# Unit 0's MoE in two halves of 128 tokens, more filler matmuls, other engines for some steps, and a new order table

## The chip, the cores and the metric

One core of a Trainium2 chip runs the whole kernel. The metric is the device time in microseconds (us) of one execution; several executions give a median. Engines are named as the profile names them: PE is TensorE (matmuls; PEld its weight loads), DVE VectorE, ACT ScalarE, POOL GpSimd, SP SyncE, which here issues the DMAs.

## The reference

For each of 4 batches and 8 heads a complex decaying state of 48 by 48 runs over 768 steps; then a feed-forward layer ("MoE" in the code) works on the joined heads.

```
scale = minimum(mag, 0.999) / (mag + 1e-06)      # mag = |a_re + i a_im|
a_re_n, a_im_n = a_re * scale, a_im * scale
for t in range(S):
    S_re, S_im = ar*S_re - ai*S_im + k_t v_t^T, ar*S_im + ai*S_re
    y[t] = q_t . S_re
x = y.transpose(0, 2, 1, 3).reshape(B * S, H * D)    # 3072 x 384
h = x @ w_in                                      # 384 -> 2048
g = h * tanh(softplus(h))
out = g @ w_out                                   # 2048 -> 384
```

## The kernel before

**Units.** The 3072 tokens are cut into 12 units of 256 tokens (three per batch), each of two chunks of 128. A unit passes four stages.

**Elementwise** (`elementwise`, L298 to L468): loads of R and I (real and imaginary decay), Q, K and V; then magnitude and phase of the decay. ScalarE does squares ("size r", "size i"), logs, exponentials, arctan and sines, VectorE the sums, the running sums over time ("scan", L391, L406), the clamp of the slope to +-1.5 (L383) and the products with q and k ("grow" L423, "turn" L447). Twelve "relay" DMAs per unit (L454) then carry the turned q and k to the layout T of the attention. Units 0 and 1 do this in two groups, one per chunk. ScalarE's functions come from two tables; `Work.act` (L161) loads the other one (an ACT_TABLE_LOAD at L164) whenever the order asks for it.

**Attention** (`attention`, L472 to L597), chunk by chunk: "kn" transposes k (L497), "am" forms the masked products (L509, L516), "y" the output in PSUM (L527), "y out" copies it to SBUF (L532), "pd", "S add" and "S fade" carry the state. Four "x move" DMAs (L577) then bring a unit's y to x, the input of the MoE; from unit 1 on x is split in a high and a low part, xH and xL (L587, L592).

**MoE** (`moe`, L599): the 2048 columns are 8 pairs of 2 x 128. For each pair "mm1" (L609) makes h in PSUM (128 partitions x 2 x 256 tokens); ScalarE does exp, square, ln and an inverse exp, VectorE a cap (L668) and the gate (L621); "mm2" (L644) adds the pair's part to two PSUM tiles po, one for each 128 tokens. In unit 0 both are plain fp32 matmuls; from unit 1 on each is three fp32r matmuls of high and low parts (gh, gl at L627, L633), with weights split likewise. "o0", "o1" copy po out and two stores from SP end the unit (L655 to L661).

**Weights** (`weight`, L240): 16 blocks (w_in and w_out of each pair by turns) come as 64-bit words in two buffers; "low" on ScalarE, "shift" and "join" on VectorE and "carry" (L264, POOL or VectorE) make fp32 of them. A block's buffer is free for the next but one after its carry. `halves` (L274) splits them for units 1 to 11 ("high", "rest").

**Order.** Each step is an operation `op(engines, name, f)`, numbered in the order in which the program lists it. The table ORDER (L49) holds these numbers in the order in which the operations are issued, with a letter where another of the allowed engines than the first is taken. Each engine, and SP's queue, works through its operations strictly in this order, so one that waits holds up all behind it. Unit 0 is listed with six "spin" operations of four matmuls of a constant (L685), whose result nobody reads.

Of the kernel before, what the change touches and what calls it, by code (L numbers as in the profile page):

```python
# [26 lines left out]
P = 128  # L27
# [3 lines left out]
C = 128  # L31
# [7 lines left out]
PLAIN = 1  # L39
SPINS, SPIN = 6, 4  # L40
# [12 lines left out]
545 136 95 91 304 132 97 133 96 99 98 93 134 305 94 135 101 324 306 542 337A 106 334 137 141 336 335 108 338 100 340  # L53
103 543 102 342 344 343 104 341 143 142 347 109 107 544 144 345 346 409 115 110 145 541 325 105 407 113 329 116 326
111 327 138 114 405 112 330 363 413 351 365 117 364 366V 367 331 352 139 349 201 348 368 140 353 546 202 350 371 203
146 151 212 355 339 411 359 358 211 357 551 204 547 361 205 221 360 213 332 548 362 206 222 214 719 147 148 720 356
549 215 369 153 207 149 216 374 552 208 150 118 217 370 152 119 375 218 223 372 154 550 156 376 224 155 554 379 120
225 209 380 226 161 377 232 158 378 417 559 159 210 227 354 157 406 539 219 724 540 160V 162 163 381 166 220 228 553
164 382 727 383 555 165 419 385 560 415 231 384 725 386 726 390 556 171 233 242 167 168 557 241 234 169 235 558 391
392 170V 243 229 172 173 176 244 569A 570A 236 174 230 245 561 393 175 237 562 246 238 423 373V 239 247 181 563 177  # L60
248 387 421 564 425 251 178 566 568 565 388 183 252 723 179 182 911 184 240 180 567 572 389 249 253 395 397 250 396
427 186 398 399 185V 575 573 401 254 261 429 402 191 579 577 255 574 262 256 576 187 188 582 400 257 189 580 263 585
403 258 190 581 264 259 578 192 583 260 910 196 193 265 584 404 266 586 194 588 587 408 267 195 590 589 268 918 592
410 915 269 916 271 197 198 433 591 272 199 917 593 437 273 200V 450 274 435 412 449 275 394 276 414 595 277 728 594
278 733 438 416 596 730 461 439 451 418 270 734 452 735 420 279 453 736 440 454 737 462 441 455 729 280 442 738 443
597 281 283 599 282 444 739 284 598 474 445A 600 731 463 446 473 732 456 464 447 457 601 475 448 458 741 459 422 740
460 476 465 424 752A 477 486 466 571 426 722 751A 602 478 721 431V 467 428 604 479 468 485 603 497 605 487 469 488 498
470 489 742 480 490 471 750 499 472 491 606 481 500 482 501 607 743 502 483 503 430 914 608 484 744 612 434 609 510
745 610 611 509 492 748 504 747 522 493 505 494 521 615V 506 749 495 616 754 511 496 507 432 756 613 617 757 523 512
# [3 lines left out]
777 931 646 629 782 778 934 780 647 935 784 930 786 783 630 648 638 787 936 656 649 639 944A 785 943 650 667 1107 640  # L73
# [3 lines left out]
695 688 800 960 1117 962 799 1105 689 1114 696 1104 1119 808 690 1106 697 806V 809 804 807 1115 698 704 805 699 703  # L77
700 963 1124 810 1125 961 705 701 1126 1127 823 1128 1118 706 1129 1289 822 1120 707 811 1130 1121 964 966 708 965 702
967 968 812 709 813 969 1123 710 814 971 711 712 970 973 815 972 713 974 824 975G 816 825 976 1122 978 714 979 1133
1131 835 826 1476 715 834 1135 827 977V 716 1134 717 817 980 828 718 1137 836 847 1132 829 982 1138 818 1139 846 837  # L80
1290 819 1141 1144 1142 858 1140 820 1143 838 981 1145 848 821 830 1146 839 983 1147 1291 831 859 1150 849 840 1136
1294 1148 832 850 1149 1483 841 833 1475 851 1296 842 860 871 1293 852 1297 1287 853 987 1286 861 989 854 843 985 862
988 1306 1298 1151 984 1295 870 855 1288 863 1307 990 882 1308 991G 986 872 995 1309 1153 864 844 993 1299 873 992
1310 845 874 994 1300 1301 856 865 875 1302 866A 857 876 867 996 894 998 877 1000 1312 999 868 878 1001 879 895 997
1303 1480 1003 1152 1481 869 1154V 1311 883 1305 1484 880 884 1486 896 1002 1304 897 885 1155 898 1316 1317 1315 886
1157 899 887 881 1156 900 1158 888 1162 1319 1313 1164 1482 1160 1668 1314 889 1320 1159 901 1321 890 1014 1322 1161V
1004 1163 1015 1165 902 891 1026 903 1016 1005 1489 892 1017 1166 1018 1326 893 1325 1006 1324 1019 904 1323 1007 1485
1329 1020 905 1008 1318 1332 1487 1490 1328 1027 1331 906 1492 908 1167 907 1009 1491 909 1327 1010A 1039 1493 1330
1028 1488 1667 1011 1038 1021 1012 1494 1478 1022A 1013 1477 1040 1023 1051 1168 1497 1029 1024 1496 1041 1498 1030
# [4 lines left out]
1182 1678 1090 1073 1681 1183 1081 1184 1334 1336 1082A 1185 1091 1083 1682 1197 1092 1684 1084 1186 1093 1683 1187  # L94
1085 1094 1188 1685 1674 1196 1095 1189 1686 1208 1190 1198 1209 1199 1687 1677 1096 1200 1679 1688 1337 1201 1339
1700A 1338 1680 1097 1340 1344 1098 1689 1690 1346 1100 1099 1202 1101 1341 1191 1342 1347 1345 1221 1192 1348G 1343
1691 1210 1220 1524 1193 1349 1351 1522 1211 1350 1194 1203 1352 1523 1212 1692 1517 1353 1222 1515 1204 1213 1223
1232 1516 1354 1224 1670 1205 1214 1357 1225 1669 1693 1215 1699A 1355 1226 1694 1854 1195 1227 1857 1356 1206 1696
1216 1228 1695 1207 1217 1701 1218 1698G 1229 1697 2041 1219 1855 1233 1244 1234 1702 1858G 1230 1856 1231 1235 1358
1245 1863 1359V 1236 1709 1360 1246 1362 1237 1257 1366 1238 1361 1247 1365 1363 1248 1525 1239 1527 1368 1249 1256  # L100
1364 1367 1859 1240A 1704 1250 1268 1241 1705 1369 1258 1861 1269 1712 1370 1862 1710 1371V 1373V 1242 1372 1671 1259
2040 1374 1711 1251 1243 1260 1703 1526V 1270 1528V 1375 1252 1860 1529 1261 1253 1531 1864 1530 1376 1271 1262 1532
1272 1263 1536 1865 1866 1538 1273 1537 1867 1388 1377 1274 1378 1264A 1387 1539 1275 1540G 1379 1265 1276A 1400 1389
1380 1533 1390 1868 1381 1541 1391 1543 1399 1392 1542V 1544 1871 1254 1869 1870 1872 1545 1873 1393 1255 1882 1874
1546 1266 1875 1277 1267 1877 1876 1278 1878 1279 1879 2233 1547 1280 1552 1282 1382 1281 1283 1534 1383 1401 1384
# [96 lines left out]
def tile_kernel(ctx, tc, q, k, v, are, aim, w_in, w_out, out):  # L202
# [38 lines left out]
    def weight(i):  # L241
# [9 lines left out]
        def low(e):  # L251
            act(word(0).bitcast(I32), word(0), AF.Copy, scale=2.0 ** -29)
# [40 lines left out]
    def wout(x, j, a):  # L293
        return x[2 * j + 1].rearrange("p (a c) -> p a c", a=2)[:, a, :]

    units = {}

    def elementwise(u):  # L298
        b, uu = divmod(u, NU)
        split = u < SPLIT_UNITS  # L300
# [171 lines left out]
    def attention(u):  # L472
# [109 lines left out]
        if u < PLAIN:  # L582
            return
# [310 lines left out]
```

## Time and profile before

| | us |
|---|---|
| median of 3 runs | 625.02 (623.94 to 625.76) |
| the profiled execution | 623.0 |
| its span, first to last instruction | 621.3 |
| PE busy | 568.6 (92%) |
| ACT busy | 507.4 (82%) |
| DVE busy | 482.2 (78%) |
| POOL busy | 42.9 (7%) |

The profiled execution is 1.7 us longer than its span (what lies around the instructions), and lies 2.0 us under the median. "Busy" counts the time in which at least one instruction ran on the engine. Matmuls are pipelined, so a busy PE need not be at its peak; their ends are modelled. The mean granted clock of the PE was 0.988 of full speed.

### The profile page before, as it was taken

Reading aid. Unit: us, or ns where it says so; the run is one execution under the profiler, and the core shown is the slowest. Engines: PE = TensorE matmul, PEld = TensorE weight load, DVE = VectorE, ACT = ScalarE, POOL = GpSimd, SP = SyncE. Lnnn points to the kernel's source line nnn. Section 1 sums busy time; section 2 is a strip of 40 time slices with the busy share of each in tenths; the row PEclk is TensorE's granted clock in tenths of the full one; section 3 lists DMA queues with packets and bytes.
Section 4 is the critical chain, followed back from the end, with each engine's and each line's share of the span. In section 5 each row is a group of like instructions: output and inputs, shape, how many; then the busy total and the mean of one; then the engine's idle time right before and its main releaser. Section 6 shows DMA issues by size and latency. Waiting matters only on the chain.

```text
span 621.3 us, 11450 instructions
## 1 busy us (share of the span) xinstructions
PE 568.6 (92%) x4394; PEld 532.8 (86%) x4394; DVE 482.2 (78%) x836; ACT 507.4 (82%) x804; POOL 42.9 (7%) x38
## 2 busy tenths in 40 slices
PE   0268987899999999999999999999999999999996
PEld 0256665689999989999999999999999999999995
DVE  5999898799998889899887976987984555353542
ACT  8999998687899999999998986899975755344780
POOL 1032231200000000000003000001000000000000
PEclk9998999799999999999999999999999999999999
DMA  8387757702543517063332433351160021020000
GB/s 292 124 245 209 210 192 221 188 26 73 130 131 94 162 61 208 15 177 114 95 100 64 119 95 111 108 142 60 47 169 16 1 78 27 1 53 1 26 1 31
DMA packets 56222, 65.46 MB, mean 105 GB/s; under 512 B 4704, under 2 KB 49760, under 8 KB 56160
## 3 DMA queue, kind: packets, MB, share of 16 engines
q1 hardware_dynamic: 56160, 64.65, 36.0%
q8 instruction: 36, 0.59, 0.4%
q14 instruction: 26, 0.21, 0.1%
HBM read 36.18 MB, written 4.72 MB: 66 GB/s over the span
## 4 chain that ended last, share of the span: by engine, by line
PE 38%; ACT 31%; DVE 15%; DMA 8%; issue 4%; SPq 3%; DVEq 0%; ACTq 0%
PE ph L609 15%; PE po L644 14%; ACT e L166 10%; ACT X L166 7%; ACT L164 6%; PE pa L509 3%; PE ypsum L527 3%; DMA T<-QK 3%; DMA x<-y 2%; DVE g L621 2%; SPq L454 2%; PE pd L539 2%; ACT R L166 2%; DMA I<-a_im 1%; DVE gl L633 1%
## 5 line engine op out<-in xcount | busy, mean ns | idle before, releaser
L609 PE MATMUL ph<-xH,wh 128*128 128x256 f32 x462 | 134.6, 291 | 1.7 <-DVE g L621 1.6
L609 PE MATMUL ph<-xL,wh 128*128 128x256 f32 x462 | 130.1, 281 | 0.0
L609 PE MATMUL ph<-xH,wl 128*128 128x256 f32 x462 | 129.8, 281 | 0.0
L166 ACT ACTIVATE e<-e 128x512 f32<-128x512 f32 x192 | 117.3, 626 | 12.6 <-DVE e L668 11.5
L644 PE MATMUL po<-wh,gh 128*128 128x384 f32 x308 | 106.7, 347 | 0.0
L644 PE MATMUL po<-wh,gl 128*128 128x384 f32 x308 | 104.7, 340 | 0.5 <-DVE gl L633 0.5
L644 PE MATMUL po<-wl,gh 128*128 128x384 f32 x308 | 104.3, 338 | 0.0
L609 PEld LDWEIGHTS ph<-xH,wh 128*128 128x128 f32 x462 | 87.2, 189 | 5.3 <-issue 1.7
L609 PEld LDWEIGHTS ph<-xL,wh 128*128 128x128 f32 x462 | 87.1, 189 | 0.2
L609 PEld LDWEIGHTS ph<-xH,wl 128*128 128x128 f32 x462 | 87.2, 189 | 0.0
L166 ACT ACTIVATE e<-ph 128x512 f32<-128x512 f32 x96 | 56.2, 591 | 32.5 <-PE ph L609 31.6
L164 ACT ACT_TABLE_LOAD x63 | 80.8, 1283 | 1.1
L621 DVE SCALAR_TENSOR_TENSOR g<-e,ph 128x512 f32<-128x512 f32 x96 | 65.0, 682 | 19.6 <-ACT e L166 18.3
L633 DVE TENSOR_TENSOR gl<-g,gh 128x512 fp32r<-128x512 f32 x88 | 60.6, 691 | 19.2 <-PE po L644 10.4
L668 DVE TENSOR_SCALAR e<-e 128x512 f32<-128x512 f32 x96 | 42.5, 443 | 36.2 <-ACT e L166 35.7
L166 ACT ACTIVATE e<-e,fifth 128x512 f32<-128x512 f32 x96 | 68.4, 719 | 1.1
L644 PEld LDWEIGHTS po<-wh,gh 128*128 128x128 f32 x308 | 57.9, 188 | 1.5 <-issue 1.5
L644 PEld LDWEIGHTS po<-wh,gl 128*128 128x128 f32 x308 | 57.9, 188 | 1.4 <-DVE gl L633 1.2
L644 PEld LDWEIGHTS po<-wl,gh 128*128 128x128 f32 x308 | 57.9, 188 | 0.0
L509 PE MATMUL pa<-T 96*128 96x128 f32 x384 | 51.2, 283 | 1.7 <-ACT kn L502 1.7
L509 PEld LDWEIGHTS pa<-T 96*128 96x128 f32 x384 | 48.1, 197 | 3.3 <-ACT kn L502 2.4
L497 PE MATMUL pkn<-ident,T 96*128 96x96 f32 x160 | 18.6, 255 | 29.4 <-DMA T<-QK 28.2
(102 smaller groups left out, 1054.9 us busy)
## 6 DMA issues: line engine op xcount, KB each, us to landing
T<-X SPq DMA_DIRECT2D x72, 129.0 KB, 2.5
T<-QK SPq DMA_DIRECT2D x72, 129.0 KB, 2.5
words<-w_in SPq DMA_DIRECT2D x8, 768.0 KB, 4.9
words<-w_out SPq DMA_DIRECT2D x8, 768.0 KB, 5.7
V<-v SPq DMA_DIRECT2D x12, 384.0 KB, 4.2
QK<-k SPq DMA_DIRECT2D x12, 384.0 KB, 4.5
QK<-q SPq DMA_DIRECT2D x12, 384.0 KB, 4.8
out_dram<-o SPq DMA_DIRECT2D x24, 192.0 KB, 2.3
```

What stands on the lines that cost most here:

```text
L164: self.nc.scalar.preload_act_table_set(need)
L166: return self.nc.scalar.activation(out, in_, func, **kw)
L454: e.dma_start(to[part * NJ + j], st[src][:, c, j])
L497: e.transpose(d["pkn", g][:, i, :], T()[:, 4 * g + i, 1, :C], ident)
L509: e.matmul(d["pa", g][:, i, :], T()[:, 4 * g + i, 1, :C], T()[:, 4 * g + i, 0, :C], start=True, stop=True)
L527: e.matmul(ypsum[64 * par:64 * par + D, i, :], lhs, rhs, start=m == 0, stop=first or m == 1)
L539: e.matmul(d["pd", g][:, i, :], d["kn"][:, h, :], st["V"][:, c, h * D:(h + 1) * D], start=True, stop=True)
L609: e.matmul(ph[j][:, a, :], win(x, j, kt, a), st[y][:, kt, :], start=n == 0, stop=n + 1 == len(todo))
L621: e.scalar_tensor_tensor(g_[j], e_[j], 2.5, ph[j], ALU.subtract, ALU.mult)
L633: e.tensor_tensor(gs[j][1], g_[j], gs[j][0].bitcast(F32), ALU.subtract)
L644: e.matmul(po[t], x[:, a, t * P:(t + 1) * P], wout(y, j, a), start=j == 0 and a == 0 and n == 0, stop=j + 1 == NPAIR and a == 1 and n + 1 ...
L668: op("V", f"{n} cap", lambda e, j=j: e.tensor_scalar_min(e_[j], e_[j], math.exp(20.0)))
```

## The change

The diff, without the order table and the parts that only pass names along:

```
-PLAIN = 1
-SPINS, SPIN = 6, 4
+PLAIN = (8, 0)
+HALVED = (0,)
+SPINS, SPIN = 40, 2
...
         def low(e):
-            act(word(0).bitcast(I32), word(0), AF.Copy, scale=2.0 ** -29)
+            if e is nc.scalar:
+                act(word(0).bitcast(I32), word(0), AF.Copy, scale=2.0 ** -29)
+            else:
+                e.tensor_scalar(word(0).bitcast(I32), word(0), 2.0 ** -29, None, ALU.mult)
...
-        op("A", f"w{i} low", low)
+        op("AV", f"w{i} low", low)
...
-                op("A", f"{n} size r", size_r)
+                op("AV", f"{n} size r", size_r)
...
-                op("A", f"{n} size i", lambda e: act(half(1), I(), AF.Square, scale=0.5))
+                op("AV", f"{n} size i", size_i)
...
-                op("V", f"{n} clamp", lambda e: e.tensor_scalar(I(), I(), -1.5, 1.5, ALU.max, ALU.min))
...
-                op("V", f"{n} turns", lambda e: e.tensor_scalar(I().bitcast(I32), x1(), INV2PI, None, ALU.mult))
+                op("VA", f"{n} turns", lambda e: act(I().bitcast(I32), x1(), AF.Copy, scale=INV2PI) if e is nc.scalar
+                   else e.tensor_scalar(I().bitcast(I32), x1(), INV2PI, None, ALU.mult))
...
-            op("A", f"{n} abs", lambda e: act(R(), I(), AF.Abs))
+            op("AV", f"{n} abs", lambda e: act(R(), I(), AF.Abs) if e is nc.scalar
+               else e.tensor_scalar(R().bitcast(U32), I().bitcast(U32), 0x7FFFFFFF, None, ALU.bitwise_and))
...
-        banks = dict(kn=("ph", 3), am=("pa", 2), pd=("po", 2)) if u == 0 else dict.fromkeys(("kn", "am", "pd"), ("pa", 2))
+        banks = {"kn": ("ph", 3) if u == 0 else ("pa", 2), "am": ("pa", 2), "pd": ("pa", 2)}
...
+        def move(ts, p0, j, r0, n):
+            def f(e):
+                y = st["y"][r0:r0 + n, :, ts].rearrange("r i t -> r (i t)") if ts == slice(0, TU) else st["y"][r0:r0 + n, :, ts]
+                e.dma_start(st["x"][p0:p0 + 4 * n, j, ts], y)
+            return f
+
+        for c, ts in enumerate((slice(0, C), slice(C, TU)) if u in HALVED else (slice(0, TU),)):
+            for r, run in enumerate(XRUNS):
+                op("S", f"u{u}{'ab'[c] if u in HALVED else ''} x move{r}", move(ts, *run))
...
+        def slot(k, j, a):
+            return 2 * (j % 2) + a if halved else a
+
+        def cols(k):
+            return slice(k[0] * C, (k[0] + 1) * C) if halved else slice(0, TU)
...
+                for a in parts:
+                    for n, (kt, x, y) in enumerate(todo):
+                        e.matmul(ph[k][:, slot(k, j, a), :], win(x, j, kt, a), st[y][:, kt, cols(k)],
+                                 start=n == 0, stop=n + 1 == len(todo))
...
+        if halved:
+            blocks = [((t, i), (2 * i, 2 * i + 1)) for i in range(NPAIR // 2) for t in range(NCH)]
+        else:
+            blocks = [((0, j), (j,)) for j in range(NPAIR)]
...
+            if halved:
+                for j in js:
+                    op("T", f"{n} mm2 {j % 2}", mm2(k, j, (0, 1), (k[0],)))
+            elif u + 1 == UNITS and js[0] + 1 == NPAIR:
+                op("T", f"{n} mm2 0", mm2(k, js[0], (0, 1), (0,)))
+                op("T", f"{n} mm2 1", mm2(k, js[0], (0, 1), (1,)))
...
-            op("S", f"u{u} store{t}", store(t))
+            op("A" if u + 1 == UNITS else "S", f"u{u} store{t}", store(t))
...
+    junk = Tiles({"junk": (ps, "po", 2, [P, 512])})
```

What it does:

- Unit 0's MoE runs as eight blocks instead of eight pairs: a block is two pairs of columns for one half (128 tokens) of the unit, again 4 x 128 values per partition. Its first matmuls have 128 columns instead of 256, and there are twice as many; its second matmuls keep shape and number. The names are u0a q0 to u0b q3.
- Unit 0's y goes to x in eight moves, four after each chunk, instead of four.
- 40 spin operations of two matmuls replace six of four, on one PSUM tile of the po pool. In the table all forty stand ahead of unit 0's first matmul.
- Unit 0's "pd" uses the PSUM pool pa instead of po.
- The clamp is gone from all units. Counted over the table, VectorE takes five of 14 size i, two of 14 size r, two of 14 abs and one of 16 low from ScalarE, and ScalarE two of 14 turns from VectorE. POOL gets a second grow and a second slope and one S fade less.
- The last pair of the last unit finishes the first 128 tokens before the second, and both its copies and its stores go over ScalarE's queue.
- The order table is new throughout: the table loads that it asks for are 59 instead of 63. Near the end of the first sixth, weight block 13 is loaded ahead of unit 1's x moves (before: after three of them) and unit 2's Q and K are loaded just ahead of that block (before: ahead of block 9).

More of the change, by code (lines that the diff above doesn't have):

```diff
@@ L296, in tile_kernel, with plain @@
     units = {}
+    def plain(u, j):
+        return u < len(PLAIN) and j < PLAIN[u]
     def elementwise(u):
@@ L597, in attention, with moe, tile_, mm1 @@
             op("V", f"u{u} xL{j}", rest(j))
-    def moe(u, st, row0, op=op, act=act, plain=False):
+    def moe(u, st, row0, op=op, act=act):
+        halved = u in HALVED
         po, ph, e_, g_, gs = {}, {}, {}, {}, {}
-        def mm1(j, a):
+        def tile_(tag, bufs, k, dtype=F32):
+            return me.tile([P, 4, C] if halved else [P, 2, TU], dtype, tag=tag, name=tag, bufs=bufs)
+        def slot(k, j, a):
+            return 2 * (j % 2) + a if halved else a
+        def cols(k):
+            return slice(k[0] * C, (k[0] + 1) * C) if halved else slice(0, TU)
+        def mm1(k, j, parts):
@@ L603, in f @@
             def f(e):
-                if j not in ph:
-                    ph[j] = ps.tile([P, 2, TU], F32, tag="ph", name="ph", bufs=3)
-                terms = [(w, "x")] if plain else [(wh, "xH"), (wh, "xL"), (wl, "xH")]
+                if k not in ph:
+                    ph[k] = ps.tile([P, 4, C] if halved else [P, 2, TU], F32, tag="ph", name="ph", bufs=3)
+                terms = [(w, "x")] if plain(u, j) else [(wh, "xH"), (wh, "xL"), (wl, "xH")]
                 todo = [(kt, x, y) for kt in range(NJ) for x, y in terms]
-                for n, (kt, x, y) in enumerate(todo):
-                    e.matmul(ph[j][:, a, :], win(x, j, kt, a), st[y][:, kt, :], start=n == 0, stop=n + 1 == len(todo))
+                for a in parts:
+                    for n, (kt, x, y) in enumerate(todo):
+                        e.matmul(ph[k][:, slot(k, j, a), :], win(x, j, kt, a), st[y][:, kt, cols(k)],
+                                 start=n == 0, stop=n + 1 == len(todo))
@@ L634, in rest, with mm2 @@
             return f
-        def mm2(j, a):
+        def mm2(k, j, parts, tokens):
             def f(e):
-                if j == 0 and a == 0:
-                    for t in range(2):
+                for t in tokens:
+                    if t not in po:
                         po[t] = ps.tile([P, 512], F32, tag="po", name="po", bufs=2)[:, :DM]
-                terms = [(g_[j], w)] if plain else [(gs[j][0], wh), (gs[j][1], wh), (gs[j][0], wl)]
-                for t in range(2):
-                    for n, (x, y) in enumerate(terms):
-                        e.matmul(po[t], x[:, a, t * P:(t + 1) * P], wout(y, j, a),
-                                 start=j == 0 and a == 0 and n == 0,
-                                 stop=j + 1 == NPAIR and a == 1 and n + 1 == len(terms))
+                terms = [(g_[k], w)] if plain(u, j) else [(gs[k][0], wh), (gs[k][1], wh), (gs[k][0], wl)]
+                for a in parts:
+                    for t in tokens:
+                        for n, (x, y) in enumerate(terms):
+                            e.matmul(po[t], x[:, slot(k, j, a), 0 if halved else t * P:C if halved else (t + 1) * P],
+                                     wout(y, j, a), start=j == 0 and a == 0 and n == 0,
+                                     stop=j + 1 == NPAIR and a == 1 and n + 1 == len(terms))
@@ L661, in store @@
             return lambda e: e.dma_start(out[ds(row0 + t * P, P), :], o[t])
-        for j in range(NPAIR):
-            n = f"u{u} p{j}"
-            op("T", f"{n} mm1 0", mm1(j, 0))
-            op("T", f"{n} mm1 1", mm1(j, 1))
-            op("A", f"{n} exp", exp(j))
-            op("V", f"{n} cap", lambda e, j=j: e.tensor_scalar_min(e_[j], e_[j], math.exp(20.0)))
-            op("A", f"{n} square", lambda e, j=j: act(e_[j], e_[j], AF.Square, bias=1.0))
-            op("A", f"{n} ln", lambda e, j=j: act(e_[j], e_[j], AF.Ln, scale=0.2, bias=fifth))
-            op("A", f"{n} inv", lambda e, j=j: act(e_[j], e_[j], AF.Exp, scale=-1.0))
-            op("V", f"{n} gate", gate(j))
-            if not plain:
-                op("VA", f"{n} gh", high(j))
-                op("V", f"{n} gl", rest(j))
-            op("T", f"{n} mm2 0", mm2(j, 0))
-            op("T", f"{n} mm2 1", mm2(j, 1))
+        if halved:
+            blocks = [((t, i), (2 * i, 2 * i + 1)) for i in range(NPAIR // 2) for t in range(NCH)]
+        else:
+            blocks = [((0, j), (j,)) for j in range(NPAIR)]
@@ new lines, in moe @@
+        for k, js in blocks:
+            n = f"u{u}{'ab'[k[0]]} q{k[1]}" if halved else f"u{u} p{k[1]}"
+            if halved:
+                for j in js:
+                    op("T", f"{n} mm1 {j % 2}", mm1(k, j, (0, 1)))
+            else:
+                for a in range(2):
+                    op("T", f"{n} mm1 {a}", mm1(k, js[0], (a,)))
+            op("A", f"{n} exp", exp(k))
+            op("V", f"{n} cap", lambda e, k=k: e.tensor_scalar_min(e_[k], e_[k], math.exp(20.0)))
+            op("A", f"{n} square", lambda e, k=k: act(e_[k], e_[k], AF.Square, bias=1.0))
+            op("A", f"{n} ln", lambda e, k=k: act(e_[k], e_[k], AF.Ln, scale=0.2, bias=fifth))
+            op("A", f"{n} inv", lambda e, k=k: act(e_[k], e_[k], AF.Exp, scale=-1.0))
+            op("V", f"{n} gate", gate(k))
+            if not plain(u, js[0]):
+                op("VA", f"{n} gh", high(k))
+                op("V", f"{n} gl", rest(k))
+            if halved:
+                for j in js:
+                    op("T", f"{n} mm2 {j % 2}", mm2(k, j, (0, 1), (k[0],)))
+            elif u + 1 == UNITS and js[0] + 1 == NPAIR:
+                op("T", f"{n} mm2 0", mm2(k, js[0], (0, 1), (0,)))
+                op("T", f"{n} mm2 1", mm2(k, js[0], (0, 1), (1,)))
+            else:
+                op("T", f"{n} mm2 0", mm2(k, js[0], (0,), (0, 1)))
+                op("T", f"{n} mm2 1", mm2(k, js[0], (1,), (0, 1)))
@@ L678, in moe @@
         for t in range(2):
             op("AV", f"u{u} o{t}", o_out(t))
-            op("S", f"u{u} store{t}", store(t))
+            op("A" if u + 1 == UNITS else "S", f"u{u} store{t}", store(t))
+    junk = Tiles({"junk": (ps, "po", 2, [P, 512])})
     def spin(e):
-        junk = ps.tile([P, 512], F32, tag="po", name="junk", bufs=2)
         for _ in range(SPIN):
-            e.matmul(junk, cmask, cmask.unsqueeze(1).broadcast_to([P, 4, P]), start=True, stop=True)
+            e.matmul(junk["junk"], cmask, cmask.unsqueeze(1).broadcast_to([P, 4, P]), start=True, stop=True)
@@ L711, in tile_kernel @@
         elementwise(u)
-        attention(u)
         if u == 0:
@@ L715, in tile_kernel @@
                 op("T", "spin", spin)
+        attention(u)
         if u == 0:
@@ L718, in tile_kernel @@
                 weight(i)
[L719 removed]
+        if u == 1:
             for i in range(NW):
@@ L723, in tile_kernel @@
             verdict()
-        moe(u, units[u], u * TU, plain=u < PLAIN)
+        moe(u, units[u], u * TU)
     with tc.manual_schedule():
```

210 lines of the change are left out of this document (108 added, 102 removed), and 25 rows, old and new, of the table ORDER.

## The prediction

> **What bounds the kernel now.** I read first the stretches (busy time of each engine in windows cut at the turns of the run; columns: window, its length, then busy us and instructions of PE, PEld, DVE, ACT, POOL, the granted clock, DMA share, GB/s).
>
> ```profile
> core 0 of [0], span 621.3 us
> core 0: us, PE busy (x) PEld busy (x) DVE busy (x) ACT busy (x) POOL busy (x), PEclk, DMA share, GB/s
> 60.00:100.00 40.00, 36.46 (x217) 26.99 (x217) 37.93 (x59) 38.14 (x58) 10.42 (x5) 1.00 0.68 211
> 100.00:116.00 16.00, 10.62 (x30) 5.91 (x29) 12.50 (x14) 9.67 (x15) 5.18 (x3) 0.79 0.95 236
> 116.00:180.00 64.00, 63.71 (x495) 59.48 (x494) 61.14 (x102) 55.67 (x88) 0.00 (x0) 1.00 0.29 85
> 180.00:320.00 140.00, 138.79 (x1138) 134.43 (x1137) 125.50 (x221) 137.28 (x212) 3.12 (x3) 1.00 0.40 114
> 320.00:460.00 140.00, 138.03 (x1150) 133.34 (x1149) 114.67 (x201) 122.55 (x190) 9.90 (x6) 1.00 0.36 101
> 460.00:616.00 156.00, 155.29 (x1191) 152.04 (x1189) 78.31 (x150) 87.97 (x152) 2.64 (x3) 1.00 0.11 29
> ```
>
> From 116 us on TensorE is never free: its idle time in the four last rows is 0.29 + 1.21 + 1.97 + 0.71 = 4.2 us of 500. So the end is the moment at which TensorE begins to be full, plus the work then left, plus a tail. Of the work left the change alters nothing (units 1 to 11 keep their matmuls). What can move the end is the run-up before 116 us, those 4.2 us, the tail, or another engine becoming the bound: from 60 to 100 us ScalarE (38.14 of 40) and VectorE (37.93) are full, and from 180 to 320 us ScalarE is (137.28 of 140).
>
> The row of 100 to 116 us is the hole: PE idle 5.4 us and at clock 0.79, ScalarE idle 6.3, VectorE 3.5, DMA share 0.95. The chain of waits says what it is made of (start, length, what):
>
> ```profile
> 99.91 0.60 SPq L577
> ...
> 101.90 5.43 DMA words<-w_out
> ...
> 109.37 6.19 DMA T<-QK
> 115.55 0.24 issue
> 115.79 0.54 PE pkn L497 x4
> ...
> 116.89 2.06 PE pa L509 x16
> ```
>
> Unit 1's x moves are issued on SyncE at 0.60 us each, behind them weight block 13 is loaded (5.43 us), behind that stand more relays of unit 2 on the queue, the last is issued at 109.37, takes 6.19 us on full DMA engines, and unit 2's first transposes (u2a kn0) start at 115.79. That is my first anchor.
>
> **The run-up in the new order.** I numbered the operations of both programs and counted the two order tables up to the same anchor. At u2a kn0 both have issued the same real TensorE work: 26 of the 32 operations of unit 0's MoE, and the attention of units 0 and 1. So the anchor's time carries straight to the end, as long as TensorE stays full behind it. The prices of ScalarE:
>
> ```profile
> L166 ACT ACTIVATE e<-e 128x512 f32<-128x512 f32 x192 | 117.3, 626 | 12.6 <-DVE e L668 11.5
> L164 ACT ACT_TABLE_LOAD x63 | 80.8, 1283 | 1.1
> L166 ACT ACTIVATE e<-e,fifth 128x512 f32<-128x512 f32 x96 | 68.4, 719 | 1.1
> L166 ACT ACTIVATE e<-ph 128x512 f32<-128x512 f32 x96 | 56.2, 591 | 32.5 <-PE ph L609 31.6
> L166 ACT ACTIVATE X<-X 128x768 f32<-128x768 f32 x30 | 25.3, 844 | 0.1
> L166 ACT ACTIVATE X<-R 128x768 f32<-128x768 f32 x30 | 25.1, 840 | 1.6 <-DVE R L391 1.6
> L166 ACT ACTIVATE X<-X,tiny 128x768 f32<-128x768 f32 x20 | 18.7, 936 | 2.1 <-POOL X L379 1.1 <-DVE X L379 0.9
> L627 ACT CAST gh<-g 128x512 fp32r<-128x512 f32 x30 | 18.4, 616 | 9.7 <-PE po L644 7.2 <-DVE g L621 2.4
> ```
>
> ScalarE ahead of the anchor: 157 instructions and loads become 154. Gone are one exp, one square and one ln of MoE (0.59 + 0.63 + 0.72 = 1.94) and three half-unit squares that go to VectorE (half of 0.84 to 0.84 each, 0.5 taken: 1.5); one y copy, one half-unit turns and two tiny copies come (1.1 by estimate, between a half-width and a full row above). Net -2.4 us. VectorE: 154 become 152. Five clamps go, three squares, one low, one join, one carry and one fade come, while a cap, a y copy and a turns go:
>
> ```profile
> L383 DVE TENSOR_SCALAR I<-I 128x768 f32<-128x768 f32 x10 | 5.5, 553 | 0.0
> ```
>
> At the mean of 60 to 100 us (37.93/59 = 0.64 each) two fewer is -1.3; clamps are cheaper than that (0.55 at most), so with what comes it may be +1.3. I take +0.5, and note that the new squares stand at the very start, where VectorE still waits for loads.
>
> SyncE and DMA: weight block 13 now stands ahead of unit 1's x moves, not behind three of them, so its 5.43 us leave the chain; but the loads of unit 2's Q and K, formerly around 75 us, stand just before it, and from the first x move to the last relay of u2a the queue holds 14 issues (13 x 0.60 = 7.8 us to the last) against 15 over 9.5 us (99.91 to 109.37). Unit 1's y copy, which lets them start, has 4.6 us less ahead of it on ScalarE by the same prices, so it comes some 4 us sooner. The turn that feeds the relays does not move by VectorE's. The last relay then goes out between 106.5 and 109 us and takes between an idle queue's 2.69 (row of 24.31 below) and 6.19: kn0 at 109 to 115, that is 0.7 to 6.8 us sooner. With ScalarE's 2.4 between, I take **3.5**. The same bytes must move, so the 0.95 doesn't vanish.
>
> **Halves, fillers, banks.** The chain over the whole run gives the rates:
>
> ```profile
> 24.31 2.69 DMA T<-QK
> ...
> 55.96 2.59 PE ph L609 x12
> ...
> 66.48 1.73 PE junk L685 x8
> ...
> 508.90 1.06 PE ph L609 x9
> ...
> 601.64 13.76 PE po L644 x78
> ```
>
> Unit 0's first matmuls go from 96 instructions of 256 columns (2.59/12 = 0.216 each, 20.7 us) to 192 of 128; the am matmuls, also plain fp32 with 128 columns, take 2.06/16 = 0.129 with their pipeline's end. 192 x 0.108 to 0.129 = 20.7 to 24.8, so 0 to +4 us on TensorE, spread over a stretch in which it idles anyway (3.5 us of 60 to 100): nothing, up to 1.5 if that cover is gone. Second matmuls and elementwise blocks keep their number and size. The Trainium skill (TensorE: Matmul & The Clock Gate, Part 3: Packing small matmuls, The mechanism) speaks against this: weight loads overlap matmuls in flight only where the row groups differ, and here each is full height. By it the doubled loads would stand bare:
>
> ```profile
> L609 PEld LDWEIGHTS ph<-x,w 128*128 128x128 f32 x96 | 17.7, 190 | 5.1 <-issue 2.6
> ```
>
> 96 more loads at 0.190 are 18 us. The chain's nine 256-column matmuls with nine different weights take 1.06 (0.118 each), less than one load's 0.190: loads do overlap here, and I keep 0.
>
> Unit 0 has four more moves, 2.4 us of SyncE; queued behind them are weight blocks 3 and 4, unit 1's K and Q. Block 3 needs block 1's buffer, which POOL's carry frees at about 40 us by count, so they are hidden. If not, weights slip by 2.4.
>
> Fillers: 80 matmuls, all ahead of u0a kn0 on TensorE. Warm they cost 1.73/8 = 0.216, 17.3 us in all; cold,
>
> ```profile
> 48.24 2.96 PE L685 MATMUL junk<-cmask 128*128 128x512 bf16 x8
> ```
>
> 0.37, 29.6. They start near 3 us (the mask is an early POOL step) and kn0 cannot start before its relay lands at 27.0. Warm they end about 22, cold about 33, 6 us late. The row of 66.48 shows the clock full once TensorE has been kept busy, so warm after the first few: 0. They save the cold start of unit 0's attention, 2 to 3 us of TensorE latency, but ScalarE and VectorE are the bound there: 0 to -1.
>
> **Behind the anchor.** At u3a am1 (one third into unit 2's MoE) the new order wants ScalarE further on: 248 against 239. A pair of grow steps (2 x 0.84), three gh casts (3 x 0.62), a table load (1.28), one exp (0.59), two output copies, an xH and a y copy (2 by estimate) come, a ln and a square (1.35) and the squares (1.5) go: about +4.6 us. VectorE is even. ScalarE idled 8.3 us of 116 to 180 and 6.3 of the hole; being 3.5 sooner and 4.6 further asks for 8.1 of those 14.6. It fits, with 6.5 over. At u3 p7 mm2 0 it is 16 more instructions and four table loads (5.1) less, again near +4; at u5 p4 mm1 0 ScalarE is one instruction and VectorE fourteen ahead (469 to 455, seven full and four half clamps among them). From there on both have room, so the 1.97 us of idle PE between 320 and 460 should shrink: **-1.0** of the 4.2 (0 to -3).
>
> **Tail.** The last matmul ends at 601.64 + 13.76 = 615.40:
>
> ```profile
> 615.42 0.93 SPq L661 DMA_DIRECT2D out_dram<-o  x2
> 615.42 0.56 DVE L657 TENSOR_SCALAR o<-po 128x384 f32<-128x384 f32 x1 [3.69 <-PE po L644]
> ```
>
> Both stores are issued after that. In the new order the first token block's sums finish six matmuls earlier (1.05 us), so its copy and store overlap the rest and only one store remains at the end: -0.5 (0 to -1).
>
> Sum: -3.5 - 1.0 - 0.5 = -5.0, span 621.3 to 616.3, this execution 623.0 to 618.0. It lies 2.0 under the median of 625.02, so the median goes to **620.0**. A measurement of this kernel tells about 0.3% (1.9 us) from no change.
>
> **Rivals.**
> Hole closed: weights 13 to 15 come before anybody asks, and PE's 5.4 idle us and its clock loss (10.62 x 0.21 = 2.2) come back, with 2 of the 4.2 and a tail of -1: -10.6, 614.4. For it: block 13 is off the chain. Against it: a DMA share of 0.95 with the same bytes. Chance 0.17.
>
> Nothing: the relays land when they did, as Q and K load in the same stretch and the turn of unit 2 is no sooner; ScalarE's +4.6 takes the idle time; only tail and a little remain: -1, 624.0. For it: VectorE's count. Chance 0.20.
>
> Slower: ScalarE becomes the bound at u3a am1. If the hole stays and ScalarE still waits there for TensorE as in 116 to 180, its +4.6 reaches TensorE, which is then idle: +4.6 - 0.5 = +4.1, 629.1. It decides when u3a am1 comes later than before. For it: 137.28 of 140 in the next stretch, so nothing is won back before 320. Against it: 14.6 idle us. Chance 0.14. Bare weight loads end there too: 18 less the 3.5 + 5.4 us of idle PE from 60 to 116 is +9, less 1.5 for tail and idle, 632.5; chance 0.02. That is what the rule of the Trainium skill named above would make of the halves.
>
> **Numbers.** Forecast 620.0, chance 0.47, own range 617 to 623. Up to 626.5 and down to 613.5 leaves out the slower cases (0.16) and little else. Faster: 0.47 + 0.17 + a little of the nothing case - a little of the forecast's end = 0.65; same 0.19; slower 0.16.
>
> **What would show it.** Right: kn0 of unit 2 at 111 to 113.5; PE idle in the stretch before it under 5 us; behind it PE idle of 3 us in 500; ScalarE idle between 116 and 180 down from 8.3 to some 3; fillers over before 25 us; unit 0's 128-column matmuls at 0.11 to 0.13 each; the last store alone in the tail. Wrong: fillers past 27 us, u3a am1 later than before with TensorE waiting for ScalarE, 128-column matmuls at 0.2 or more.

## The result, and the profile after

The changed kernel takes 621.26 us (median of 12 runs, 618.96 to 622.90); the kernel before took 625.49 us beside it (12 runs, 623.94 to 628.33). The ratio is 0.9925, 95% interval 0.9907 to 0.9942: some 0.7% faster, 4.2 us by the medians where 5.0 were forecast.

The profiled executions lie closer together: 621.72 us (span 620.0) against 623.0 (span 621.3). Before's profile is of a run 2.5 us under its kernel's median, the changed kernel's of one 0.5 us above its own. So the traces can show 1.3 us of the 4.2, and a second profile of each was taken below.

The stretches of the changed kernel, cut as before (window, length, busy us and instructions of PE, PEld, DVE, ACT, POOL, then clock, DMA share, GB/s):

```profile
60.00:100.00 40.00, 35.39 (x275) 28.84 (x273) 37.38 (x61) 37.00 (x58) 11.43 (x5) 0.98 0.62 192
100.00:116.00 16.00, 9.63 (x39) 6.52 (x40) 14.47 (x16) 11.77 (x18) 1.89 (x1) 0.90 0.88 238
116.00:180.00 64.00, 64.00 (x503) 60.25 (x502) 61.78 (x99) 60.51 (x99) 2.44 (x1) 1.00 0.39 112
180.00:320.00 140.00, 139.30 (x1136) 134.36 (x1135) 122.77 (x217) 133.10 (x204) 10.63 (x4) 1.00 0.38 106
320.00:460.00 140.00, 140.00 (x1167) 134.96 (x1165) 113.14 (x200) 117.47 (x179) 13.75 (x7) 1.00 0.35 99
460.00:616.00 156.00, 153.76 (x1182) 150.34 (x1180) 80.98 (x152) 89.83 (x153) 3.22 (x3) 1.00 0.12 32
```

The hole of 100 to 116 us is still there: TensorE idles 6.4 us in it (5.4 before). Behind it TensorE's idle time is 0.00, 0.70 and 0.00 (before: 0.29, 1.21, 1.97); the 2.24 of the last row are the tail, as its last matmul ends at 613.8 (615.4 before). ScalarE's idle time from 116 to 180 us fell from 8.3 to 3.5.

The chain of waits in the run-up (start, length, what):

```profile
44.87 4.30 PE ph L641 x24
...
92.97 2.96 PE ph L641 x24
...
102.70 7.72 DMA x<-y
...
110.44 0.41 ACT xH L607
110.85 0.54 ACT e L168
...
111.41 0.70 DVE g L654
...
112.16 4.54 PE po L678 x8
116.70 0.66 PE pkn L515 x8
117.36 2.71 PE ph L641 x24
```

Unit 0's MoE starts before 45 us and not at 55.8, yet unit 2's first transposes (u2a kn0, 116.5 us where they start in the trace) come no sooner than the 115.79 of before. Before, a relay was last there. Now it is a move of unit 1's x, issued on SyncE behind weight block 14 and 7.72 us on its way. In ScalarE's order the xH of this x stands ahead of an exponential of unit 0, so VectorE's gate g and eight second matmuls of 0.57 each (the clock is at 0.62 of full speed from 112 to 116.5 us) wait behind it.

What TensorE waits for between 116 and 613 us, in the waits (waiting group <- what ended last: us in total, times, longest). Before:

```profile
PE ph L609 <- DVE g L621: 1.6, 3, 0.8
PE po L644 <- DVE gl L633: 0.8, 2, 0.5
PE pkn L497 <- DMA T<-QK: 0.5, 1, 0.5
PE po L644 <- DVE gh L627: 0.4, 1, 0.4
PE pa L509 <- ACT kn L502: 0.2, 1, 0.2
PE pd L539 <- DVE am L516: 0.2, 1, 0.2
```

and after:

```profile
PE pa L527 <- ACT kn L520: 0.3, 1, 0.3
PE ph L641 <- DVE g L654: 0.2, 1, 0.2
```

Of the 3.2 us that are gone, 2.6 are waits for VectorE's g, gl and gh, the gate and its rounding that feed the second matmuls.

### The profile page after: what moved, and what is told of

Same layout as the page of the kernel before. It is cut to its first block, busy times and chain, and to the rows that moved or that the text cites. A ratio compares the mean times of both kernels' runs of the same rounds, so it can differ in the third digit from the quotient of the medians.

```text
span 620.0 us, 11717 instructions
## 1 busy us (share of the span) xinstructions
PE 589.3 (95%) x4546; PEld 548.6 (88%) x4546; DVE 480.3 (77%) x828; ACT 502.9 (81%) x793; POOL 55.2 (9%) x39
## 4 chain that ended last, share of the span: by engine, by line
PE 71%; ACT 14%; DVE 6%; DMA 4%; issue 2%; SPq 1%; POOL 1%; ACTq 0%; DVEq 0%; POOLq 0%
PE ph L641 27%; PE po L678 27%; PE ypsum L545 6%; PE pa L527 6%; ACT X L168 4%; ACT e L168 4%; PE pd L557 3%; ACT L166 3%; DMA words<-w_out 2%; PE pkn L515 1%; DMA x<-y 1%; POOL w L269 1%; SPq L472 1%; ACT words L168 1%; DMA QK<-q 1%
## 5 line engine op out<-in xcount | busy, mean ns | idle before, releaser
L527 PE MATMUL pa<-T 96*128 96x128 f32 x384 | 52.7, 284 | 3.1 <-ACT kn L520 2.5
L534 DVE TENSOR_TENSOR am<-pa,cmask 128x512 f32<-128x512 f32 x48 | 32.9, 686 | 17.8 <-PE pa L527 17.7
```

What stands on the lines that cost most here:

```text
L527: e.matmul(d["pa", g][:, i, :], T()[:, 4 * g + i, 1, :C], T()[:, 4 * g + i, 0, :C], start=True, stop=True)
L534: e.tensor_tensor(d["am", g], d["pa", g], cmask.unsqueeze(1).broadcast_to([P, 4, C]), ALU.mult)
```

## The experiments

The question was what carries the gain, since the run-up, the largest term of the forecast, did not move. Four theories stood against each other. **Cold run-up** (the expectations call it A, and B its denial: the engines and the transfers set the run-up): TensorE's clock is at half for much of 24 to 62 us (0.66 of full speed from 27 to 60 us, 0.90 before), which eats what the new order wins there; keep it warm and u2a kn0 comes sooner. **Hole** (C): the transfers between 96 and 116 us set u2a kn0 and with it the end. **Engines behind** (D): VectorE and ScalarE behind u2a kn0 hold the end as well, so the end follows the order there. **Engine work** (E, against it F, the order alone): the twelve moved operations and the lost clamps bring the gain, in any order. Beside these: are the halves worth something, and the tail?

The two kernels and all twelve runs; kn0 is the start of u2a kn0, am1 that of u3a am1, "last" the end of the last matmul, each from the run's trace:

| run | median us | ratio to before, 95% | kn0 | am1 | last | span |
|---|---|---|---|---|---|---|
| before | 625.49 | | 115.8 | 177.0 | 615.4 | 621.3 |
| before_again | 623.99 | 0.9981 [0.9952, 1.0009] | 115.4 | 176.6 | 615.7 | 622.2 |
| changed kernel | 621.26 | 0.9925 [0.9907, 0.9942] | 116.5 | 177.7 | 613.8 | 620.0 |
| after_again | 619.69 | 0.9918 [0.9886, 0.9949] | 115.5 | 178.1 | 613.7 | 620.1 |
| nofill | 621.16 | 0.9941 [0.9913, 0.9969] | 115.6 | 177.7 | 613.9 | 618.4 |
| fill96 | 619.90 | 0.9919 [0.9886, 0.9951] | 115.6 | 177.5 | 612.8 | 618.8 |
| warm | 622.82 | 0.9948 [0.9921, 0.9975] | 116.9 | 178.1 | 615.9 | 620.3 |
| hole | 621.12 | 0.9925 [0.9898, 0.9951] | 114.1 | 179.3 | 615.0 | 619.4 |
| clamp | 622.35 | 0.9947 [0.9923, 0.9971] | 116.2 | 178.5 | 613.6 | 619.4 |
| engines | 624.07 | 0.9962 [0.9931, 0.9992] | 119.2 | 180.4 | 618.2 | 622.6 |
| whole | 634.44 | 1.0140 [1.0112, 1.0168] | 130.1 | 192.5 | 628.2 | 632.4 |
| before_moves | 626.26 | 1.0025 [0.9990, 1.0059] | 115.3 | 176.5 | 616.1 | 621.9 |
| before_lean | 624.64 | 0.9987 [0.9960, 1.0014] | 114.7 | 175.9 | 615.3 | 621.1 |
| tail | 620.99 | 0.9913 [0.9881, 0.9944] | 118.2 | 179.9 | 615.3 | 621.2 |

### The two kernels again

No edit in either.

> The changed kernel once more, for a second profile and as the partner of the runs beside it. Its first profile has unit 2's first transposes (u2a kn0) at 116.7 us against 115.8 before: the 3.5 us that the prediction gave to the run-up are not in it. Theory A, cold run-up: TensorE stood at half clock from 24.1 to 30.9, 37.7 to 48.0 and 51.4 to 61.6 us, and that swallowed them; in another execution the half-clock stretches lie elsewhere and kn0 with them, between 112 and 118. Theory B, full engines: ScalarE, VectorE and the DMAs set the run-up, kn0 stays within 1 us of 116.7. Both: ratio to the kernel before 0.991 to 0.994.

> The kernel before, unchanged, for a second profile. 625.6. If its first profile was one with a long tail (5.9 us) but otherwise short, the second shows unit 2's first transposes at 116 to 117, unit 7's fourth block at 420 to 421 and the last matmul's end at 616 to 618 instead of 615.4. If the first profile was typical: 115.8, 419.4 and 615.4 within 0.7 us, and the 4.2 us between the medians lie in how often a tail is long, not in what the profiles show up to the last matmul.

The changed kernel's second median is 1.6 us under its first, and that of the kernel before 2.2 us under the 626.20 measured beside it. So 1.5 to 2 us between two medians say nothing by themselves; the intervals do. The marks repeat: the last matmul ends at 615.4 and 615.7 before, at 613.8 and 613.7 after. That is 1.8 us of gain which does not hang on the tail. kn0 by itself scatters more: 116.5 and 115.5 here, and 118.2 in the run "tail", whose program is the same up to the last unit.

### Fillers and the cold run-up

nofill:

```
-SPINS, SPIN = 40, 2
+SPINS, SPIN = 40, 0
```

> The changed kernel with none of its filler matmuls (each spin operation issues nothing). Theory A: the attention of unit 0 starts cold from its first matmul, some 3 us of TensorE time more before 45 us, and the end comes 1 to 3 us later than with fillers (ratio 0.994 to 0.998). Theory B: the fillers end before anything real starts and the run-up is set by others: no difference to after_again beyond 0.2%. The prediction gave the fillers 0 to 1 us.

fill96 (the last eight of the forty spins issue four matmuls each, so that fillers end near 25.3 us):

```
-        for _ in range(SPIN):
+        spun.append(1)
+        for _ in range(SPIN if len(spun) <= 32 else 2 * SPIN):
```

> The changed kernel with 96 fillers instead of 80 (the last eight spins have four matmuls each), so that they end at about 25.3 us, where unit 0's first transposes start (25.2), not at 21.8. Theory A: the clock does not fall at 24.1; unit 0's chunk a attention takes 4 us instead of 8, u0a y1 ends near 29.5 instead of 32.5, and the end comes 1 to 3 us sooner than in after_again (ratio 0.987 to 0.991). Theory B: same as after_again within 0.2%. If the fillers hold up the first transposes, 0.5 us later at most.

warm (fill96, and 48 more fillers ahead of seven operations of the run-up):

```
+FILL = {"u0b pd0": 8, "u0b y0": 4, "u0b y1": 4, "u0a q0 mm1 1": 4, "u0b q0 mm1 0": 16, "u0a q1 mm1 0": 8, "u0b q0 mm1 1": 4}
...
+                for _ in range(FILL.get(name, 0)):
+                    self.fill()
```

> fill96 and 48 more fillers put ahead of operations of unit 0 for which TensorE waited in the profile (u0b pd0 8, u0b y0 and y1 4 each, u0a q0 mm1 1 4, u0b q0 mm1 0 16, u0a q1 mm1 0 8, u0b q0 mm1 1 4), so that the clock stays full from 10 to 62 us. Theory A: unit 0's halved first matmuls take 1.3 us instead of 2.9, the run-up gets 3 to 5 us shorter, ratio 0.983 to 0.988. Theory B: the fillers cost nothing and bring nothing, ratio as after_again within 0.2%; where a filler stands in the way of work that was ready it costs up to 0.8 us each, 1 to 3 us in all.

The stretch of 27 to 60 us, in the changed kernel

```profile
27.00:60.00 33.00, 25.36 (x167) 23.06 (x166) 28.20 (x44) 28.56 (x48) 8.07 (x4) 0.66 0.62 184
```

and in warm:

```profile
27.00:60.00 33.00, 29.60 (x202) 21.31 (x201) 25.96 (x43) 27.14 (x46) 8.04 (x4) 0.84 0.60 172
```

The clock went from 0.66 to 0.84, ScalarE and VectorE did not do more in those 33 us but less (27.14 and 25.96 against 28.56 and 28.20), and kn0 came at 116.9. Warming the run-up by fillers gains nothing, though the fillers queue ahead of real matmuls, so by this run alone the clock's own share isn't separated. The two profiles of the changed kernel help there, as they have the same program: the clock of this stretch is 0.66 in the first and 0.55 in the second, and the colder one reaches kn0 first (116.5 and 115.5). Without any filler kn0 stands at 115.6 and the last matmul ends at 613.9; the median, 621.16, lies 0.1 us under the changed kernel's first and 1.5 above its second. So the fillers as a whole are worth nothing that these runs show, and nothing here makes the cold run-up the cause of the time.

### The hole

hole (tokens of the order table moved; the loads of unit 3's V and unit 4's I leave the stretch):

```
-... u3 V load, u1 x moves, w14 load, u4 I load, u2a relays ..., w15 load ...
+... u1 x moves, w14 load, u2a relays ... sin1, u3 V load, ..., w15 load, u4 I load ...
```

> The changed kernel with two loads that nobody needs soon moved behind the relays on SyncE's queue: unit 3's V behind the last relay of u2a, unit 4's I behind weight block 15. In four profiles of the changed kernel and of its filler variants u2a kn0 starts at 115.5 to 116.9 us whatever came before it. Theory C, DMA hole: it waits for relays that share the DMA engines with 1.5 MB of such loads; without 0.8 MB of them it starts at 112 to 114 and, TensorE being full behind it, the end comes 1.5 to 3.5 us sooner than in after_again (ratio 0.986 to 0.989). Theory D, engines: VectorE, ScalarE and the weights hold the stages behind kn0, so kn0 comes sooner but u3a am1 stays at 177.5 to 178.2 and the end is the same within 0.2%.

kn0 came 2.4 us sooner (114.1) than in the changed kernel's first profile. The eight second matmuls ahead of it show what made the lead, in that profile, in the second one and in hole:

```profile
112.16 4.54 PE L678 MATMUL po<-w,g 128*128 128x384 f32 x8 [4.57 <-DVE g L654]
112.25 2.85 PE L678 MATMUL po<-w,g 128*128 128x384 f32 x8 [3.15 <-DVE g L654]
110.89 2.85 PE L678 MATMUL po<-w,g 128*128 128x384 f32 x8 [3.15 <-DVE g L654]
```

Against the first profile 1.7 us are the granted clock (0.62 there, full here) and 1.3 the late x move, less 0.5 behind the matmuls, mostly a wait for a relay. The second profile has the full clock too, with both loads still in the stretch, and there it takes as long from the first x move to kn0 as in hole: 13.9 us (101.6 to 115.5, and 100.25 to 114.1). So it is not shown that the two loads move kn0 at all; the 1.4 us between these two are there at the first x move already.

The end did not follow the sooner kn0: am1 came 1.6 us later and the last matmul 1.2 later than in the first profile, with the median as it was. TensorE's stretches show where the lead went:

```profile
124.00:128.00 4.00, 2.54 (x18) 1.50 (x18) 2.53 (x5) 4.00 (x9) 1.66 (x1) 0.83 0.01 2
128.00:132.00 4.00, 4.00 (x11) 2.22 (x10) 4.00 (x7) 3.88 (x7) 0.00 (x0) 0.75 0.00 0
```

and the chain of waits of the same kernel names the order of events:

```profile
123.36 0.85 ACT X L168
124.21 1.66 ACT e L168 x3
...
125.89 0.70 DVE g L654
...
126.63 7.10 PE po L678 x16
```

Being early, TensorE ran into ScalarE and VectorE: it waited for the gate g until 126.6, and then the clock fell (0.83 and 0.75 here, 1.00 in the changed kernel from 120 us on), so that sixteen second matmuls took 7.10 us, against 5.43 in the changed kernel. A sooner kn0 alone is worth nothing here; the engines behind it have a date of their own. Other runs bear this out: in the seven with kn0 between 114.1 and 116.9 (both of the changed kernel, nofill, fill96, warm, hole, clamp) these sixteen matmuls start between 126.2 and 127.1.

### Halves

whole (unit 0's MoE undivided under the same table; ten of its operations that now lacked their inputs stand later, and the four moves stand where those of the second half stood):

```
-HALVED = (0,)
+HALVED = ()
```

> The changed kernel with unit 0's MoE undivided: eight pairs of 256 tokens, first matmuls of 256 columns, four x moves; the order table is kept, ten operations of unit 0 that would come ahead of their inputs wait until these are issued. Theory D: unit 0's MoE has slack either way, kn0 at 115 to 117, ratio within 0.3% of after_again. The prediction priced the halves at nothing on TensorE (0 to 4 us, hidden), and their gain at nothing of its own. A theory that the halves are what brought the gain: 3 to 6 us later, ratio 0.998 to 1.003.

13.2 us slower than the changed kernel by the medians, and all of it is there at kn0 (130.1, 13.5 us later). Neither theory of the expectation came true. The waits of TensorE between 60 and 180 us in it:

```profile
PE po L677 <- DVE g L653: 8.4, 4, 4.8
PE ph L640 <- POOL w L268: 6.9, 2, 4.2
```

Unit 0's first MoE matmul starts at 54.7 instead of 44.7, and the gates and weights that the table's places were made for come late. What this shows is that the table can't do without the halves. It is no price of halves by themselves: the table was made for them, and the old table without them is only 4 us slower.

### Clamps and moved operations

clamp (the limit to ±1.5 is put back behind the slope on VectorE):

```
+                nc.vector.tensor_scalar(I(), I(), -1.5, 1.5, ALU.max, ALU.min)
```

> The changed kernel with the clamp back, right behind each unit's slope on VectorE (14 instructions, 6.9 us of VectorE by the rows of before). Theory E, relief: the stalls of TensorE between 320 and 460 us (1.97 us idle before, 0.0 now) went because VectorE and ScalarE have room; with the clamp back some come again, and the end is 1 to 3 us later than after_again (ratio 0.993 to 0.996). Theory F, order: the new table removed them; the clamp fits in VectorE's idle time, same within 0.2%.

engines (the twelve letters taken off the table: five size i, two size r, two abs, one low back on ScalarE, two turns back on VectorE):

> The changed kernel with the twelve moved steps back on their old engines (five size i, two size r, two abs and one low on ScalarE, two turns on VectorE), same order. Theory E: ScalarE gets some 6 us more to do and was full from 180 to 320 us: the end is 1 to 4 us later than after_again (ratio 0.993 to 0.998), most of it already there at u3 p7 mm2 0. Theory F: same within 0.2%.

before_moves (the twelve letters, and the code behind them, in the old order of the kernel before; nothing else):

> The kernel before in its own old order, with only the changed kernel's twelve moved operations (five size i, two size r, two abs and one low to VectorE, two turns to ScalarE). Putting these twelve back cost the changed kernel 3.6 us (624.07 against 620.5, the mean of its two medians). If the moves by themselves bring the gain: 625.6 - 3.6 = 622, unit 2's first transposes at 115.8 - 2 = 113 to 114. If it is the new order that gains and the moves only fit that order: 624.5 to 626, those transposes at 115 to 116. A rival: the old order's VectorE pays for them (five squares, two abs and a low at some 0.8 each, 37.93 busy of 40 between 60 and 100 us): 626.5 to 628.

before_lean (before_moves without the fourteen clamps):

```
-                op("V", f"{n} clamp", lambda e: e.tensor_scalar(I(), I(), -1.5, 1.5, ALU.max, ALU.min))
```

> The kernel before in its old order with the twelve moves and without the clamp on the slope (fourteen VectorE operations fewer, 0.28 to 0.55 us each). If engine work carries the gain and order and halves do not: 620 to 621, as the changed kernel. If order and halves carry it: 624 to 626. In between (622 to 623): about half of the gain is engine work that any order would have had.

clamp is 1.1 and 2.7 us slower by its median than the changed kernel's two, its interval overlaps with theirs, and its last matmul ends 0.2 us sooner than in the first profile. Its ratio lies where theory E put it, but the stalls that E expected back did not come: TensorE is busy for 140.00 of the 140 us from 320 to 460. So no price of the clamps is shown. Putting the moves back costs the new order 2.8 and 4.4 us by the changed kernel's two medians, with intervals that touch (0.9931 to 0.9992 and 0.9907 to 0.9942). In the profile the last matmul ends 4.4 later, 2.7 of that at kn0 already, which one profile cannot tell from the scatter of kn0. But in the old order the same moves bring nothing (1.0025 [0.9990, 1.0059]), and with the clamps gone as well 0.9987 [0.9960, 1.0014]. So "engine work in any order" fell. The waits of TensorE behind the hole in before_moves

```profile
PE po L658 <- DVE gl L647: 1.4, 3, 0.8
PE ph L623 <- DVE g L635: 1.3, 3, 0.6
PE pkn L511 <- DVE gl L647: 0.6, 1, 0.6
PE pd L553 <- DVE am L530: 0.2, 1, 0.2
```

and in before_lean

```profile
PE po L656 <- DVE gl L645: 2.2, 3, 1.5
PE ph L621 <- DVE g L633: 0.5, 1, 0.5
PE pd L551 <- DVE am L528: 0.4, 1, 0.4
PE po L656 <- DVE gh L639: 0.2, 1, 0.2
```

(both from 119 to 613 us) are those of the kernel before: 3.5 and 3.3 us, still for g and gl above all, against 0.5 in the new order (1.6 in its second profile, 1.5 in engines). Fewer VectorE instructions don't remove them; another order, with the halves that belong to it, does. The time from kn0 to the last matmul's end says the same: 499.6 to 500.8 us in the four profiles of the old order, 497.1 to 499.0 in nine of the ten of the new one (engines 499.0, clamp 497.4), and 500.9 in hole.

### The tail

tail (the last second matmuls in the old order, both stores on SyncE, the second copy on VectorE):

```
-            elif u + 1 == UNITS and js[0] + 1 == NPAIR:
-                op("T", f"{n} mm2 0", mm2(k, js[0], (0, 1), (0,)))
-                op("T", f"{n} mm2 1", mm2(k, js[0], (0, 1), (1,)))
...
-op("A" if u + 1 == UNITS else "S", f"u{u} store{t}", store(t))
+op("S", f"u{u} store{t}", store(t))
```

> The changed kernel with the tail of before: the last second matmuls in the old order, both stores on SyncE, the second block's copy on VectorE. If the new tail gains what the prediction said, 0.5 us: 621.0 against 620.5 and 0.5 us more from the last matmul's end to the span's end. If it gains nothing (5.9 us before, 6.2 after in the profiles, with values near 4.4 in other profiles of the same tail): 620 to 621, and the time from the last matmul to the end is again near 4.4 or near 6, by how long the last store's transfer takes (2.0 or 3.5 to 4.0 us), whatever the order. Price of a worse tail in the change: then 619.5 to 620.

By the median it can't be told from the changed kernel (620.99). The profiles tell more, if all are taken together. From the last matmul's end to the span's end the old tail took 5.9, 6.4, 5.9, 5.9 and 5.9 us (before, before_again, before_moves, before_lean, tail); the new one took 6.2, 6.4 and 6.0, 5.8 in four profiles and 4.3 to 4.5 in five. The end of the changed kernel (start, length; the second store stands alone):

```profile
613.28 0.38 ACTq L695 DMA_DIRECT2D out_dram<-o  x1
...
613.84 0.49 ACT L689 ACTIVATE o<-po 128x384 f32<-128x384 f32 x1 [0.59 <-PE po L678]
614.37 0.34 ACTq L695 DMA_DIRECT2D out_dram<-o  x1
```

The second store is issued 0.6 us after the last matmul in both orders (614.37 after 613.76 here, 616.01 after 615.39 before). It took 3.78 us to land here, 3.52 before and 2.01 in nofill: that, and not its place, made the changed kernel's profiled tail 0.3 us longer than before's. Of the new tail's landings five are near 2.0 and four at 3.4 to 4.0; the five of the old tail lie at 2.9 to 4.3. Whether the new order is what lets some be short, so few profiles can't say.

## Why the prediction was right, and where not

**The time** was right, 621.26 for 620.0; the sum was not made of the parts that were forecast. Its largest term failed, a smaller one came out twice as large, and a part of the measured gain has no place, so that the total came so close is in part luck.

**Run-up, -3.5: failed.** It was +0.7 at kn0 in the two profiles compared, +0.4 as the mean of two each. Of the signs named for it, kn0 at 111 to 113.5 and TensorE idle under 5 us ahead of it, neither came (116.5 and 6.4). The work that ScalarE lost became idle time. ScalarE's waits from 27 to 100 us before

```profile
ACT X L166 <- DVE R L391: 1.3, 1, 1.3
ACT R L166 <- DVE I L412: 0.7, 1, 0.7
ACT kn L502 <- PE pkn L497: 0.6, 2, 0.3
```

and after:

```profile
ACT e L168 <- PE ph L641: 3.9, 2, 2.7
ACT y L550 <- PE ypsum L545: 1.6, 1, 1.6
ACT words L168 <- DMA words<-w_out: 0.8, 1, 0.8
ACT wh L285 <- POOL w L269: 0.7, 1, 0.7
```

2.6 us became 7.2 (0.2 more than the rows shown): 4.6 more, as much as the prediction had counted less ahead of unit 1's y copy. 3.9 of the 7.2 are waits for unit 0's own first matmuls, which the new order puts ahead of other work as early as 45 us. The step that counted ScalarE's instructions up to the anchor and took the difference as time left out that ScalarE now waits for TensorE there. So the y copy came at 99.5 us (99.3 before), not 4 us sooner. Weight block 13 did leave the chain (issued at 96.6 us in place of 101.9), and the x moves behind it met the loads of unit 2's Q and K, of block 14 and of unit 3's V, as the text had half feared: the longest of them took 7.72 us. The last relay for kn0 landed at 115.96 us, 115.55 before. The prediction had kn0 wait for that relay alone; it left out unit 0's second matmuls just ahead of kn0, whose gate was late in the first profile and which ran at the lower clock there. In the second profile, at full clock, kn0 does wait for the relay, 0.4 us, and that one lands at 115.4, between the 115.55 and 115.2 of the two profiles before.

**"The anchor's time carries straight to the end": right for later, wrong for sooner.** Where kn0 came later than in the changed kernel (tail +1.7, which is scatter and not its edit, engines +2.7, whole +13.5) the last matmul came 1.5, 4.4 and 14.4 later. Where it came sooner it did not (hole -2.4 gave +1.2; after_again, nofill and fill96, 0.9 to 1.0 sooner, gave -0.1, +0.1 and -1.0).

**Halves, 0 (0 to +4): the price was right.** Twenty-four 128-column matmuls take 2.96 and 2.71 us on the chain (0.12 and 0.11 each), and 4.30 (0.18) where the clock was at 0.50 from 44 to 48 us. The weight loads for them, in the instructions of one line (ns, least/median/most):

```profile
L641 PEld LDWEIGHTS ph<-x,w x192: 186/192/337, 44.6 to 119.7; 128*128 128x128 f32 x192
```

take longer, 0.192, than a matmul with its load costs in the warm chain, so they overlap the matmuls before them. The Trainium skill (TensorE: Matmul & The Clock Gate, Part 3: Packing small matmuls, The mechanism) says in one sentence that loads overlap only where the row groups differ; these are of full height, so this trace disagrees with that sentence, as the prediction took it. The same section also names a background weight buffer as a second way, which would not disagree.

**Fillers, 0 to -1: right.** They run to 21.8 us at 0.25 each:

```profile
L735 PE MATMUL junk<-cmask 128*128 128x512 bf16 x80 | 20.0, 418 | 1.7 <-POOL cmask L222 1.7
```

nofill shows no worth of them. That they save unit 0's attention a cold start was wrong, since TensorE then waits until 25.2 for its first transposes and the clock is at 0.66 from 27 to 60 us; it cost nothing that warm could win back.

**ScalarE behind the anchor: right.** Its idle time from 116 to 180 us fell to 3.5 (some 3 forecast). The slower rival's sign came by half: am1 is later than before, by 0.7 and 1.5 us in the two pairs of profiles, but of TensorE's waits behind kn0 only 0.3 us are for ScalarE.

**TensorE's idle time behind the anchor, -1.0 (0 to -3): right in kind, the size was twice that.** From kn0 to the last matmul's end it took 499.6 and 500.3 us before, 497.2 and 498.2 after: -2.2. VectorE's lead of fourteen instructions at u5 p4 was named as the reason; the waits that went are indeed those for VectorE, and before_lean shows that it is the place in the order, not the number of VectorE's instructions.

**Tail, -0.5: not shown.** From the last matmul to the end it is 6.0 in the mean of the five profiles of the old tail, 5.2 in the nine of the new: -0.8, with a scatter of 2. That an earlier copy and store shorten the end, as forecast, is not in it: the last store goes out 0.6 us after the last matmul in both. The difference lies in how long the store takes to land.

With the tail's mean these make +0.4 - 2.2 - 0.8 = -2.6. The medians say -4.2, the shortest runs of all -3.0 (621.79 and 618.77, in the run of after_again): some 1.6 us of the gain stay without a place. The kernel before is longer in most unprofiled executions (its medians are 624.0 to 626.2) than in its two profiles (623.0 and 624.0). A part of that goes with the clock: of its 86 executions that have a clock on record, the 26 with a mean granted clock of 0.992 or more have a median of 623.9 us, the other 60 one of 626.7. That is no proof, as its first profile has 0.988 and 623.0, and no run here sets the clock alone.

## What to carry to other kernels

Count the work ahead of an anchor, and then ask whom each engine waits for in the new order: most of what ScalarE saved turned into waiting for the very matmuls that were pulled forward. A lead at one point is worth something only if the engines behind it are early too, while a delay there costs in full; so test an anchor from both sides. And a move of work between engines is worth what the order makes of it: by the medians the same twelve moves brought some 3 to 4 us in one table and nothing in the other. And compare one profile with a second one of the same kernel before reading a difference into it: kn0 moved by 2.7 us between profiles of one run-up.

## What the runs showed of the hardware that was not expected

The last store of the new tail, always of the same size, takes 1.9 to 2.1 us from issue to landing in five profiles and 3.4 to 4.0 in four (nofill 614.54 to 616.55, after 614.37 to 618.15); that alone moves a run by 1.5 to 2 us.

In hole the granted clock fell to half at 126.6 us and stayed there for 3.4 us, though TensorE had idled only 1.8 us of the 8 from 120 to 128 us. The Trainium skill (TensorE: Matmul & The Clock Gate, Part 1: The HAM clock gate, What's actually happening) has the clock fall after an idle window of about 3.4 us; here a stretch that was idle in part was enough, which disagrees with the page. The same idle time did not always end in the same way: 3.15 us ahead of the eight second matmuls before kn0 left the clock full in the changed kernel's second profile (2.85 us for the eight), 3.16 in nofill did not (4.54 us).

The fourth move of unit 1's x, issued right behind a weight block in both orders, took 7.72 us to land in the changed kernel's first profile, 6.2 in its second, 5.4 before and 4.6 in hole. The first of the four, with the same bytes and issued ahead of that block, took 2.69 before (99.91 to 102.60) and 4.3 after.
